# The order of the steady periods of attention: the first values behind the scores, the router's product behind the transposes of q and k

## The chip, the cores and the metric

One core of a Trainium2 chip runs the program. The time is device microseconds of one execution; the time before is the median of three executions, 636.98 us (636.5 to 638.11). A difference of about 0.3% (1.9 us) can be told from none.

## The reference

Attention in chunks of 64 tokens feeds a mixture of experts, where each token goes through one expert of eight:

```python
scores = scale * q_c @ k_c.T           # per batch, head, chunk of 64; head dimension 64
attn = exp(scores - max) / (sum + 1e-9)
out = attn @ v_c                       # 8 x 8 x 576 x 64
x = out as (8, 576, 512)
logits = x @ w_gate; local_gate = sigmoid(x @ w_local)
# e: argmax of the logits, or the previous token's expert where local_gate >= 0.5
h = maximum(x[b, s] @ w1[e], 0)
result[b, s] = softmax(logits)[e] * (h @ w2[e])
```

## The kernel before

The 4608 tokens are cut into 18 blocks of 256. Attention works on several blocks at once, as a pipeline written out by hand: a string of names per stage says in which order the instructions of PE, DVE, ACT and POOL are put into their queues, and each engine runs its queue in that order. The blocks 1 to 15 give fifteen equal periods, which all play the string `PAR["steady"]`; ahead of them stands `PAR["start"]`, behind them `PAR["drain"]`, and then the experts run tile by tile until 638 us.

In period i the names stand for the following (`name*n` takes the next n pieces of that name):

- `s`: the scores of block i+1 (eight pieces of small 64x64 products on PE, L216), then the row maxima on DVE (L227), the subtraction on DVE (L230), the exponential on ACT (L235)
- `va`: the values of block i-1, two halves of four pieces of 64x65 products on PE (L265), each half followed by its division by the row sums on DVE (L277 to L279); both halves use the same PSUM tile `o`, of which there is one
- `tx`: eight 128x128 transposes on PE (L179) of the finished block i-2, in two groups of four; each group fills one of three PSUM tiles `tr`, and ACT copies it out (L169)
- `tq`: sixteen such transposes of q and k of block i+2, in four groups of four, copied out by ACT into `qkT`
- `ra`: the router of block i-2 in four pieces: a product with 32 output rows on PE (L307), a copy `lT` on DVE (L312), two transposes on PE (L316), a reduction on DVE (L321) which four small copies on POOL follow (L325, tile `L`)
- `pr`: four copies on POOL (L171), which pair the heads of block i+3's q and k
- `tp`: eight transposes on PE of the probabilities of block i, two groups, copied out by ACT into `pT`, which the values of the next period read
- `w`: from period 13 on a part of the first expert's weights is split, on ACT (L932) and POOL (L933)
- `lq`, `lv`: the loads of q, k and v for later blocks, on SP's queue
- `h0` to `h3`: in the periods 11 to 15 pieces of the routing of the first 18 tiles, by the numbers in `PAR["hooks"]`: sorting on DVE, small transposes on PE, at the end the one-hot tiles `rh` (L450; six on DVE at h2 of period 14, twelve on POOL at h3), the product of these on PE (L588, h2 of period 15), from which DVE makes the indices and POOL gathers the first tiles of the experts (L627)

```python
    man = tc.manual_schedule(engines=MAN | {ET.Pool})
    for i in range(1, NS - 2):
        play(" ".join(toks), qs4 | {k: v for k, v in opt.items() if v is not None})
```

Period 1 has no `tx` and no `ra`. SP's queue is not in the string's hands: its instructions follow the program.

Of the kernel before, what the change touches and what calls it, by code (L numbers as in the profile page):

```python
# [59 lines left out]
    "t0": "VAVA",  # L60
    "t1": "AAAA",
    "t2": "AVAA",
    "steady": "lq s*8 s h0 tx*8 s va*4 va tq*8 ra*2 h1 tq*8 pr*4 w*4 va*4 lv va ra*2 h2 tp*8 s h3 ",
    "stores": {5: (0,), 6: (1,), 7: (2,), 8: (3,), 9: (4,), 10: (5,), 11: (6,), 12: (7,), 13: (8,), 14: (9,), 15: (10, 11)},
    "hooks": [45, 45, 47, 47, 49, 49, 50, 50, 51, 51, 53, 53, 54, 57, 58, 59, 61, 62, 62],
}
# [1217 lines left out]
```

## Time and profile before

| | |
|---|---|
| median of three runs | 636.98 us |
| the profiled execution, its own time | 640.15 us |
| span of the trace | 638.4 us |
| PE busy | 595.9 us, 93% of the span |
| DVE, ACT, POOL busy | 59%, 50%, 41% |
| granted clock of TensorE, mean | 0.987 of 2.4 GHz |
| steady periods 2 to 15 in the trace | 30.86 to 147.47 us |

The page lists each engine's busy time, groups of instructions and waits. More is read here from the order of time: which instruction an engine starts when, and what ended the idle time ahead of it. Times are counted from the span's start. The trace's counts of matmuls are of issued instructions: a float32 product of 64 columns counts twice, so the 16 products of one half of the values stand as x32.

### The profile page before, as it was taken

Reading aid. Unit: us, or ns where it says so; the run is one execution under the profiler, and the core shown is the slowest. Engines: PE = TensorE matmul, PEld = TensorE weight load, DVE = VectorE, ACT = ScalarE, POOL = GpSimd, SP = SyncE. Lnnn points to the kernel's source line nnn. Section 1 sums busy time; section 2 is a strip of 40 time slices with the busy share of each in tenths; the row PEclk is TensorE's granted clock in tenths of the full one; section 3 lists DMA queues with packets and bytes.
Section 4 is the critical chain, followed back from the end, with each engine's and each line's share of the span. In section 5 each row is a group of like instructions: output and inputs, shape, how many; then the busy total and the mean of one; then the engine's idle time right before and its main releaser. Section 6 shows DMA issues by size and latency. Waiting matters only on the chain. (4 is left out here: it accounts for less than half of the span.)

```text
span 638.4 us, 16143 instructions
## 1 busy us (share of the span) xinstructions
PE 595.9 (93%) x5313; PEld 467.4 (73%) x5313; DVE 378.2 (59%) x813; ACT 318.3 (50%) x546; POOL 263.5 (41%) x559
## 2 busy tenths in 40 slices
PE   4898999888998999999999999999999999999992
PEld 3776887766776878677888786768868688687772
DVE  1665667886686476667535366773666744565330
ACT  2665777656521245675424366653565633545320
POOL 3432433476335234364542353644354445324201
PEclk9998999989998999999999999999999999999997
DMA  9999999998754366597947487969599894559301
GB/s 207 267 215 243 240 283 242 285 251 251 255 179 133 85 101 203 105 310 155 193 97 95 97 208 150 277 144 182 166 138 290 176 198 86 119 169 225 67 18 40
DMA packets 148657, 114.03 MB, mean 179 GB/s; under 512 B 105616, under 2 KB 125072, under 8 KB 148496
## 3 DMA queue, kind: packets, MB, share of 16 engines
q1 hardware_dynamic: 141856, 91.43, 61.5%
q0 software_dynamic: 6640, 20.65, 12.0%
q8 instruction: 77, 1.26, 0.8%
q14 instruction: 84, 0.69, 0.4%
HBM read 77.28 MB, written 20.35 MB: 153 GB/s over the span
## 5 line engine op out<-in xcount | busy, mean ns | idle before, releaser
L700 PE MATMUL y<-w2h,hp 128*128 128x512 f32 x560 | 184.5, 399 | 2.5 <-DVE hp L624 1.0
L686 PE MATMUL h<-w1h,xp 128*128 128x512 f32 x560 | 158.8, 393 | 0.1
L868 POOL DMA_INDIRECT out<-ysb,sidx x41 | 44.1, 1076 | 225.6 <-issue 72.4
L700 PEld LDWEIGHTS y<-w2h,hp 128*128 128x128 f32 x560 | 105.6, 189 | 25.2 <-DVE hp L624 1.4
L686 PEld LDWEIGHTS h<-w1h,xp 128*128 128x128 f32 x560 | 104.1, 188 | 24.8 <-ACTq L1067 1.6
L700 PE MATMUL y<-w2l,hp 128*128 128x512 f32 x280 | 110.0, 393 | 1.4 <-DVEq L1067 1.3
L686 PE MATMUL h<-w1l,xp 128*128 128x512 f32 x280 | 86.7, 391 | 1.5 <-DVEq L1067 1.5
L169 ACT COPY hw<-h 128x512 uint16<-128x512 uint16 x60 | 32.2, 589 | 88.6 <-PE h L686 83.6
L171 POOL COPY qk<-qk 128x512 f32<-128x512 f32 x69 | 40.2, 617 | 60.9 <-issue 31.3
L171 DVE COPY hw<-h 128x512 uint16<-128x512 uint16 x60 | 38.6, 685 | 41.2 <-PE h L686 39.9
L686 PEld LDWEIGHTS h<-w1l,xp 128*128 128x128 f32 x280 | 52.2, 188 | 13.5 <-DVEq L1067 2.2
L700 PEld LDWEIGHTS y<-w2l,hp 128*128 128x128 f32 x280 | 53.0, 189 | 12.3 <-DVEq L1067 2.4
L179 PE MATMUL tr<-ident,qk 128*128 128x128 f32 x288 | 43.7, 299 | 10.9 <-ACT qk L169 5.5
L169 ACT COPY qkT<-tr 128x512 f32<-128x512 f32 x69 | 37.6, 589 | 30.5 <-PE tr L179 25.1
L775 ACT COPY hsb<-ht 128x512 uint16<-128x512 uint16 x58 | 41.5, 775 | 17.6 <-DMA ht<-hw 8.3
L627 POOL DMA_INDIRECT xg<-x_d,gidx x39 | 45.6, 1170 | 9.5 <-issue 4.4
L864 DVE TENSOR_SCALAR ysb<-y,ppr 128x512 f32<-128x512 f32 x35 | 26.2, 749 | 37.5 <-DVEq L1067 21.6
L179 PEld LDWEIGHTS tr<-ident,qk 128*128 128x128 f32 x288 | 34.4, 152 | 18.8 <-POOL qk L171 9.1
L779 DVE SCALAR_TENSOR_TENSOR hp<-hsb,hp 128x512 fp32r<-128x512 f32 x58 | 37.6, 690 | 14.4 <-ACT hp L778 14.4
L106 DVE TENSOR_TENSOR w2l<-raw,w2h 128x1024 fp32r<-128x1024 f32 x28 | 32.5, 1220 | 15.9 <-ACT w2h L105 13.8
L778 ACT ACTIVATE hp<-hsb 128x512 fp32r<-128x512 f32 x58 | 33.5, 623 | 10.1 <-DVE hsb L776 9.0
L227 DVE TENSOR_REDUCE mx<-sc 128x8 f32<-128x512 f32 x36 | 23.1, 684 | 22.5 <-PE sc L216 22.5
(237 smaller groups left out, 872.4 us busy)
## 6 DMA issues: line engine op xcount, KB each, us to landing
raw<-in_moe_w SPq DMA_DIRECT2D x28, 1024.0 KB, 6.4
raw<-in_moe_w SPq DMA_DIRECT2D x16, 512.0 KB, 5.7
qk<-in_q SPq DMA_DIRECT2D x11, 512.0 KB, 6.2
qk<-in_k SPq DMA_DIRECT2D x11, 512.0 KB, 7.1
v<-in_v SPq DMA_DIRECT2D x22, 256.0 KB, 6.1
x_d<-xs SPq DMA_DIRECT2D x7, 521.0 KB, 6.6
x_d<-x_w2h SPq DMA_DIRECT2D x6, 521.0 KB, 6.3
x_d<-x_w2l SPq DMA_DIRECT2D x5, 521.0 KB, 8.1
```

The source lines that it names most:

```text
L106: (lo_eng or nc.vector).tensor_tensor(lo, raw, hi.bitcast(F32), ALU.subtract)
L169: eng.copy(dst, src)
L171: eng.tensor_copy(dst, src)
L179: nc.tensor.transpose(box["ps"][:, n], src_of(n), ident)
L627: nc.gpsimd.indirect_dma_start(out=dst, out_offset=None, in_=src, in_offset=bass.IndirectOffsetOnAxis(ap=gidx[t].bitcast(U32), axis=0))
L686: nc.tensor.matmul(hs[j], xs[a][:, c], W1[w][c][:, 512 * j:512 * j + 512], start=(c == 0 and n == 0), stop=(c == 3 and n == 2))
L700: nc.tensor.matmul(y, hx[f // 4][a][:, f % 4], W2[w][c][:, f % 2, :], start=(f == 0 and n == 0), stop=(f == 7 and n == 2))
L775: nc.scalar.copy(bits[:, j, :, :, 1], ht[:, j, 1])
L778: nc.scalar.activation(hp[j][:, 0], full[:, j], AF.Relu)
L779: V.scalar_tensor_tensor(hp[j][:, 1], full[:, j], 0.0, hp[j][:, 0].bitcast(F32), ALU.max, ALU.subtract)
L864: either(kind and kind[1], lambda: V.tensor_scalar(ysb, y, pr, None, ALU.mult), lambda M: y_part(ysb, y, pr, M), True)
L868: nc.gpsimd.indirect_dma_start(out=out, out_offset=bass.IndirectOffsetOnAxis(ap=sidx[t].bitcast(U32), axis=0), in_=ysb, in_offset=None, bo ...
```

## The change

The string of the steady periods changes, and nothing else. The first half of the values (`va*4`) moves from behind `tx` to right behind the scores; the router's product and its copy (`ra*2`) move from between the two halves of `tq` to behind `pr` and `w`, ahead of the second half of the values; the router's transposes and reduction (the second `ra*2`) move from ahead of the hook h2 to behind `tp`.

```diff
-    "steady": "lq s*8 s h0 tx*8 s va*4 va tq*8 ra*2 h1 tq*8 pr*4 w*4 va*4 lv va ra*2 h2 tp*8 s h3 ",
+    "steady": "lq s*8 s h0 va*4 tx*8 s va tq*8 h1 tq*8 pr*4 w*4 ra*2 va*4 lv va h2 tp*8 ra*2 s h3 ",
```

On PE, in period 2, between the scores of block 3 and the scores that follow (x_w2h is the finished block in its ring buffer, `qk_505` and so on are the four groups of q and k, `pr` the probabilities), there stands before:

```order
L179 MATMUL tr<-ident,x_w2h 128x128 x8
L265 MATMUL o<-v_112,pT 64x65 x16
L179 MATMUL tr<-ident,qk_505 128x128 x4
L179 MATMUL tr<-ident,qk_506 128x128 x4
L307 MATMUL lg<-xT,wg_72 32x256 x4
L179 MATMUL tr<-ident,qk_507 128x128 x4
L179 MATMUL tr<-ident,qk_508 128x128 x4
L265 MATMUL o<-v_112,pT 64x65 x16
L316 MATMUL lg<-ident,lT 128x128 x2
L179 MATMUL tr<-ident,pr 128x128 x8
```

and now:

```order
L265 MATMUL o<-v_112,pT 64x65 x16
L179 MATMUL tr<-ident,x_w2h 128x128 x8
L179 MATMUL tr<-ident,qk_505 128x128 x4
L179 MATMUL tr<-ident,qk_506 128x128 x4
L179 MATMUL tr<-ident,qk_507 128x128 x4
L179 MATMUL tr<-ident,qk_508 128x128 x4
L307 MATMUL lg<-xT,wg_72 32x256 x4
L265 MATMUL o<-v_112,pT 64x65 x16
L179 MATMUL tr<-ident,pr 128x128 x8
L316 MATMUL lg<-ident,lT 128x128 x2
```

The first values now follow the scores without transposes between them, and twenty-four transposes stand in a row; the same holds in every period from 2 to 15.

On DVE, at h2 of period 14 (the second division, the six one-hot tiles, the router's reduction of that period, and the maxima of the next scores), there stands before:

```order
L277 TENSOR_SCALAR rs<-o 128x8
L278 RECIPROCAL rs<-rs 128x8
L279 TENSOR_TENSOR x_w2l<-o,rs 128x2x256
L321 TENSOR_REDUCE x_w2l<-lg 128x2x9
L450 TENSOR_SCALAR rh<-iota_m,rq 128x128 x6
L227 TENSOR_REDUCE mx_2807<-sc_2773 128x8
```

and now:

```order
L277 TENSOR_SCALAR rs<-o 128x8
L278 RECIPROCAL rs<-rs 128x8
L279 TENSOR_TENSOR x_w2l<-o,rs 128x2x256
L450 TENSOR_SCALAR rh<-iota_m,rq 128x128 x6
L321 TENSOR_REDUCE x_w2l<-lg 128x2x9
L227 TENSOR_REDUCE mx_2807<-sc_2773 128x8
```

The reduction has moved behind the one-hot tiles. Likewise in the periods 11 to 15 the copy `lT` (L312) now stands behind the DVE work of h1, where it stood ahead of it. ACT's and SP's queues hold the same instructions in the same order.

## Rows read from the trace of the kernel before

**Rows 1.** Busy time by stretch: length, engines' busy us, granted clock, DMA share, GB/s.

```profile
47.27:58.69 11.42, 9.07 (x171) 7.43 (x170) 5.14 (x14) 5.35 (x10) 3.09 (x8) 0.85 1.02 251
73.15:80.37 7.22, 7.22 (x172) 5.93 (x171) 4.98 (x14) 5.25 (x10) 3.10 (x8) 1.00 0.99 240
102.99:110.47 7.48, 7.48 (x174) 6.09 (x173) 5.97 (x17) 5.52 (x11) 2.97 (x7) 1.00 0.90 204
110.47:119.03 8.56, 7.88 (x176) 6.23 (x175) 7.35 (x23) 5.77 (x12) 3.81 (x11) 1.00 1.12 286
127.61:135.47 7.86, 7.29 (x172) 5.94 (x171) 7.20 (x23) 6.05 (x12) 4.36 (x10) 1.00 1.04 240
```

**Rows 2.** Timeline of PE, period 7: start, us, instruction, count, [idle before <-what ended it].

```profile
73.14 1.16 PE L216 MATMUL sc<-qkT 64*64 64x64 f32 x64
74.24 1.09 PE L179 MATMUL tr<-ident,x_w2l 128*128 128x128 f32 x8
75.26 0.70 PE L265 MATMUL o<-raw,pT 64*64 64x65 f32 x32
75.89 1.09 PE L179 MATMUL tr<-ident,qk 128*128 128x128 f32 x8
76.91 0.64 PE L307 MATMUL lg<-xT,wg 128*32 128x256 f32 x8
77.48 1.09 PE L179 MATMUL tr<-ident,qk 128*128 128x128 f32 x8
78.50 0.70 PE L265 MATMUL o<-raw,pT 64*64 64x65 f32 x32
79.13 0.44 PE L316 MATMUL lg<-ident,lT 128*128 128x128 f32 x2
79.40 1.04 PE L179 MATMUL tr<-ident,pr 128*128 128x128 f32 x8
80.37 0.34 PE L216 MATMUL sc<-qkT 64*64 64x64 f32 x8
```

**Rows 3.** Timeline of PE, period 1, where values follow scores.

```profile
25.05 0.68 PE L265 MATMUL o<-raw,pT 64*64 64x65 f32 x31
```

**Rows 4.** Timeline of ACT, period 7: the copies of two `tr` tiles.

```profile
74.98 1.07 ACT L169 COPY xT<-tr 128x512 f32<-128x512 f32 x2
```

**Rows 5.** Timeline of PE, 26.9 to 51 us: waits early in the kernel.

```profile
26.95 2.33 PE L179 MATMUL tr<-ident,qk 128*128 128x128 f32 x16 [1.23 <-POOL qk L171]
...
40.59 0.71 PE L265 MATMUL o<-v,pT 64*64 64x65 f32 x4
42.17 0.68 PE L265 MATMUL o<-v,pT 64*64 64x65 f32 x28 [0.87 <-DMA v<-in_v]
...
50.53 0.56 PE L216 MATMUL sc<-qkT 64*64 64x64 f32 x19 [2.35 <-issue]
```

**Rows 6.** Timeline of DVE, period 11: first operation of h1, first behind it.

```profile
108.02 0.29 DVE L362 TENSOR_REDUCE mxb<-L 128x18 f32<-128x144 f32 x1
...
110.12 0.16 DVE L277 TENSOR_SCALAR rs<-o 128x8 f32<-128x8 f32 x1
```

**Rows 7.** Timeline of DVE, end of period 14.

```profile
135.81 0.22 DVE L321 TENSOR_REDUCE x_w2l<-lg 128x18 f32<-128x72 f32 x1
135.95 2.20 DVE L450 TENSOR_SCALAR rh<-iota_m,rq 128x128 bf16<-128x128 bf16 x6
```

**Rows 8.** Timeline of POOL, periods 14 and 15.

```profile
137.39 1.05 POOL L325 COPY L<-x_w2l 64x9 f32<-64x9 f32 x4
138.54 7.06 POOL L450 TENSOR_SCALAR rh<-iota_m,rq 128x128 bf16<-128x128 bf16 x12
```

**Rows 9.** Timeline of PE, period 15 and the drain.

```profile
139.08 0.33 PE L216 MATMUL sc<-qkT 64*64 64x64 f32 x4 [2.46 <-issue]
...
146.01 0.60 PE L588 MATMUL tr<-qv,rh 128*128 128x6 bf16 x18
...
158.20 0.63 PE L621 MATMUL tr<-ident,raw 128*128 128x128 f32 x4 [1.37 <-DMA raw<-x_d,gidx]
```

## Prediction, made before the changed kernel ran

> **What bounds the kernel now.** I read the busy times by stretch first, then PE's timeline of one plain period, then every wait of PE from 26 to 160 us, and last the queues that release those waits. A plain period (4 to 10) takes 7.22 us, and PE is busy through all of it, while DVE, ACT and POOL have 5 us of work or less [rows 1]. So PE's own sequence sets the pace there; what the reader is to see in its timeline is that it holds no wait, only blocks of three shapes (128x128 transposes, 64x64 products, the 32-row router product) that alternate [rows 2]. Elsewhere something else is last. In period 3 PE waits for v of block 2 until 42.17, and at 50.53 it has lost 2.35 us to nothing that the profile shows [rows 5]. In period 12 DVE has 7.35 us of work in 8.56 [rows 1]. In periods 14 and 15 POOL's twelve one-hot tiles end at 138.54 + 7.06 = 145.60, and PE uses them at 146.01 [rows 8, 9]. From there a chain over DVE and POOL leads to the gather, for which PE waits 1.37 us at 158.20 [rows 9].
>
> **The change part by part.** No work is added or removed. All of it is order.
>
> *Scores and first values together.* From start to start, the scores with 64 instructions take 74.24 - 73.14 = 1.10 us and a half of the values with 32 takes 75.89 - 75.26 = 0.63 [rows 2]. The difference, 0.47, is what 32 instructions more cost where the shape stays. In period 1, where values follow scores, they run on with no idle time ahead of them [rows 3]. So the two together take 1.10 + 0.47 = 1.57 instead of 1.73, and 0.16 us is saved. Their inputs are there: ACT has copied the probabilities' transposes half a microsecond before, since the scores stand between.
>
> *Twenty-four transposes in a row.* Eight alone take 75.26 - 74.24 = 1.02. The ten of router and probabilities, in a row today, take 80.37 - 79.13 = 1.24 [rows 2]; so a transpose within a row costs 0.11. Twenty-four in a row take 1.02 + 16 x 0.109 = 2.76 instead of 3 x 1.02 = 3.06, and 0.30 is saved. The probabilities and the router's two still stand together, in the other order, at the same 1.24. The router's product now has values behind it, not transposes: its 77.48 - 76.91 = 0.57 [rows 2] I keep. No row shows that neighbour; I bound it by 0.07 either way, what the product's own 0.64 and the 0.57 to the next start lie apart.
>
> *What the row costs.* Three `tr` tiles serve six groups. ACT copies one in 0.59 and starts the next 0.48 later (1.07 for two), its first 74.98 - 74.24 = 0.74 after the row begins [rows 2, 4]; PE makes a group in 4 x 0.109 = 0.44. The fourth group would start at 1.36, its tile is free at 0.74 + 0.59 = 1.33; after that ACT falls behind by 0.05 a group. I take 3 x 0.05 = 0.15. The other end is the sixteen transposes at 26.95, which took 2.33 for four groups [rows 5], 0.56 a group instead of 0.44; they followed POOL's copies, and with their pace the row would lose 5 x 0.12 = 0.6, more than all that is saved. I take the low end, as ACT's copies here are the nearer row.
>
> So a plain period gains 0.16 + 0.30 - 0.15 = **0.31 us** (0.46 at most, a loss of 0.14 at worst), and falls to 6.91.
>
> *Period 3.* The values now come before `tx`, at about 39.1, and v lands just ahead of 42.17, whatever PE does: its load stands in SP's queue in period 1. Today PE does `tx` in that time and waits 0.87 at the end [rows 5]. Now it waits 3 us and does the transposes afterwards. From 42.17 the rest of the values takes 0.5, then the remaining 6.91 - 1.57 = 5.3 of the period: the next scores start at about 48.1, not at 47.27. The lead of period 2 is gone and 0.8 us besides. Seven plain periods (4 to 10) at 0.31 then give 2.2; period 11 begins 1.4 us early.
>
> *Periods 11 to 13.* DVE's work of h1 now stands ahead of `lT`. In period 11 it is 110.12 - 108.02 = 2.1 us [rows 6]; `lT` ends some 7.2 us into the period, the two router transposes were due at 6.6 in a 6.91 period, so PE waits about 0.7 and the period takes 7.8 with the hook's own transposes, against 7.48 [rows 1]: a loss of 0.35. Period 12 goes by DVE, as before; shorter waits for the tile `o` give some 0.45 back (0 to 0.8). Period 13 gains the 0.3 of a plain one. Period 14 starts 1.8 us early.
>
> *Periods 14 and 15.* This is the dearest part. The reduction L321 now stands behind DVE's six one-hot tiles, 2.20 us [rows 7]. POOL's queue holds the four copies that read the reduction, and behind them its twelve one-hot tiles, 7.06 us [rows 8]. Today the reduction starts 135.81 - 127.61 = 8.20 into period 14 and POOL ends the tiles at 145.60, 17.99 into it. Now it starts at 10.4 or, with `lT` late, up to 11; the copies take 1.05, and the tiles end 18.9 to 19.6 into the period: 0.9 to 1.6 lost, I take 1.3. PE came 146.01 - 145.60 = 0.41 late to them [rows 9] because of 2.46 us of waiting at 139.08; now it stands waiting and follows at once, 0.4 won. That wait is over 3 us. The one of 2.35 at 50.53 was followed by a stretch at half clock, 1.2 GHz: period 4 has a granted clock of 0.85 and took 11.42 - 7.22 - 2.35 = 1.85 more than wait and work [rows 1, 5]. The like here costs 1.85, of which the 1.37 that PE waits for the gather covers most: 0.5 lost.
>
> Sum: 1.8 - 1.3 + 0.4 - 0.5 = **0.4 us** gained at the gather. Behind it every stage hangs on PE, 93% busy, and moves with it. Against the profiled execution that is 640.15 - 0.4; that execution is 0.5% above the median of the runs, so I carry the 0.4 to the median: **636.6 us**.
>
> **The rivals.**
>
> *Faster, the wait on nothing goes.* In period 4 PE lost 2.35 and 1.85 of half clock [rows 1, 5]. The profile names no cause; DMA is at 1.02 there. If PE, held in period 3, reaches that place late enough, 4.2 us go: 632.4. For it: the wait is a matter of moments. Against it: the same instructions come in the same traffic.
> What the row shows is a 2.35 us wait of PE in straight-line code. The Trainium skill's page Runtime: NRT & Kernel Launch, section Instruction fetch mechanics, says that instructions are fetched in blocks by DMA while others run, and calls the cost of a block's border mostly hidden. By that rule such a wait would cost nothing and this rival and the one of its like below would go; no row names the fetch, and 2.35 us is not hidden.
>
> *Faster, POOL's chain has room.* If the one-hot tiles are not what PE waits for (the gather's landing then moves with PE), 1.3 + 0.5 come back, and with the full 0.46 a period 7 x 0.15 = 1.0 more: 633.8. Against it: 146.01 follows 145.60 closely [rows 8, 9].
>
> *Slower, half clock at both new waits.* The wait of period 3 becomes 3 us, with but four instructions in it, longer than the 2.35 that drew the half clock. It decides whether it counts as idle as that one did: then 1.85 falls due there, and if the wait for the gather gives no cover at L588, 1.37 more: 636.6 + 3.2 = 639.8.
>
> *Slower, one wait more like that of period 4.* DMA share is 0.9 to 1.12 in these periods [rows 1], and PE uses its instructions 4% faster: 636.6 + 4.2 = 640.8.
>
> *Slower, the row of transposes waits on `tr`.* With the pace of 26.95 nothing of the 0.31 is left in eight periods: 636.6 + 2.5 = 639.1. It decides at 0.46 us of waits a period.
>
> **How the numbers follow.** About 0.3% (1.9 us) is what a measurement can tell, so 635.1 to 638.9 is no change. The forecast has 0.45, with a range of its own of 635.1 to 638.5, from 0.46 or 0.15 a plain period, 0.9 or 1.6 at POOL, 0 or 0.8 in period 12. The first faster rival has 0.15, the second 0.12, the half clock 0.15, one wait more 0.07, the `tr` tiles 0.06. So faster 0.27, same 0.45, slower 0.28. Those of 632.4 and 640.8 lie at the range's edges: 632.3 to 640.2 leaves out half of the first and all of the second with the tails of the others, some 2 in 10.
>
> **What would show it.** A plain period of 6.9 us with scores and values as one block, and PE with no wait ahead of the later groups of the row (else the `tr` rival). PE idle from 39 to 42 us, and the clock's rows behind it. A reduction L321 behind the one-hot tiles, POOL's copies waiting for it, PE waiting over 3 us ahead of L588. Wrong would be a lead at the end of period 13 that arrives in full at the gather, or a plain period that is not shorter.

## The result, and the profile of the changed kernel

The changed kernel takes 646.69 us (median of six runs, 641.53 to 649.52), the kernel before beside it 637.55 (634.54 to 640.02): 1.0135 times as long, 95% interval 1.0085 to 1.0184. It is slower by 9 us, where no change was forecast, and outside the range.

The stretches, as in [rows 1] (length, busy us of PE, PEld, DVE, ACT, POOL, granted clock, DMA share, GB/s), for the periods 3, 4, 5, 10, 12, 13 and 14:

```profile
38.75:51.59 12.84, 10.58 (x171) 9.12 (x170) 5.26 (x13) 5.55 (x11) 3.21 (x8) 0.73 1.08 254
51.59:59.38 7.79, 7.33 (x171) 6.01 (x170) 5.15 (x13) 5.07 (x11) 3.03 (x8) 1.00 0.92 239
59.38:66.40 7.02, 7.02 (x172) 5.83 (x171) 5.21 (x13) 5.07 (x11) 3.04 (x8) 1.00 0.80 228
96.58:107.57 10.99, 8.79 (x171) 7.60 (x170) 5.20 (x13) 5.26 (x11) 3.03 (x8) 0.84 1.01 222
115.30:125.17 9.87, 7.85 (x175) 6.26 (x174) 7.20 (x22) 5.23 (x11) 3.25 (x9) 1.00 1.09 289
125.17:135.64 10.47, 9.04 (x173) 7.73 (x172) 6.65 (x18) 5.74 (x11) 4.16 (x9) 0.84 0.56 147
135.64:145.14 9.50, 7.30 (x171) 5.81 (x170) 9.19 (x23) 7.58 (x14) 6.93 (x12) 1.00 0.83 207
```

A plain period without a wait is indeed shorter, 7.02 instead of 7.22. But period 10, which has the same work, takes 10.99, and 12 and 13 some 10. Two profiles of each kernel (the second ones are of the runs a1 and b1 below) give the sums, in us:

| periods | before | before, second | after | after, second |
|---|---|---|---|---|
| 2 to 4 | 27.83 | 24.42 | 27.58 | 26.42 |
| 5 to 13 | 68.91 | 73.06 | 76.25 | 77.31 |
| 14 and 15 | 19.86 | 18.72 | 21.71 | 21.49 |
| from there to the end | 490.9 | 488.5 | 487.6 | 486.4 |

The profiled executions are 6.7 us apart on the mean. What periods 14 and 15 lose, 2.3 on the mean, the stages behind them give back. The loss that stays is in the periods 5 to 13: 5.8 us on the mean, where the prediction had a gain. PE's timeline shows what it is made of (start, us, instruction, count, [idle before <-what ended it]):

```profile
74.94 0.58 PE L216 MATMUL sc<-qkT 64*64 64x64 f32 x25 [0.56 <-issue]
90.64 0.56 PE L265 MATMUL o<-v,pT 64*64 64x65 f32 x18 [0.86 <-issue]
99.57 0.63 PE L216 MATMUL sc<-qkT 64*64 64x64 f32 x27 [2.20 <-issue]
117.92 0.62 PE L265 MATMUL o<-v,pT 64*64 64x65 f32 x26 [1.34 <-issue]
126.92 0.90 PE L216 MATMUL sc<-qkT 64*64 64x64 f32 x41 [1.17 <-issue]
```

These are waits like that of 50.53 in [rows 5], for nothing that the profile names: 6.13 us in the periods 5 to 13 (7.52 in the second profile), and in each profile two stretches of 3.4 us at half clock (granted 0.5 of 2.4 GHz) behind them, which cost 1.7 each by estimate (half of 3.4). That is 10.2 us on the mean. In the kernel before it is 0.95 and 3.94, and no half clock there. One wait more of each of its profiles belongs to them, though the profile puts it down to DVE:

```profile
101.75 0.44 PE L316 MATMUL lg<-ident,lT 128*128 128x128 f32 x2 [0.41 <-DVE rs L277]
```

```profile
103.94 0.44 PE L316 MATMUL lg<-ident,lT 128*128 128x128 f32 x2 [1.51 <-DVE x_w2h L279]
```

The second is of the second profile, where `lT` was ready at 101.49; the next part shows by the count of instructions what PE waited for. With these two it is 3.4 us on the mean. Waits and half clock taken out, the nine periods last 67.55 and 67.61 us before, 66.72 and 66.39 after. So the change gained 1.0 us there, and 6.8 us more of waits and half clock turn that into the loss of 5.8.

### Where these waits stand

PE's records (matmuls, weight loads, and the waits and other instructions of its sequencer) can be counted from the first. In 20 profiles (both kernels and all the runs below) 98 waits of PE on nothing of 0.15 us and more lie between 30 and 160 us. 96 of them stand at a record that is 193 or 194 past a multiple of 256; the other two lie behind 154 us. The waits at 101.75 and 103.94 stand at 194 too. The profile's table of DMA queues has two rows for instructions, and one of them is (packets, MB, share):

```profile
q8 instruction: 77, 1.26, 0.8%
```

1.26 MB in 77 packets is 16,384 bytes each, 64 for each of 256 instructions, and up to 160 us there is one packet for each such block of PE. The records of packets give, for the profile of the changed kernel and some of the runs below:

```
kernel               PE goes on   wait   packet began ahead of that   after the border before
before                 50.53      2.35   2.78                         5.39
before                139.08      2.46   2.38                         5.71
after                  90.64      0.86   2.29                         2.40
after                  99.57      2.20   2.40                         6.53
after                 126.92      1.17   2.64                         6.36
d3_after_shifted      133.34      5.18   2.53                         6.73
```

In all 96 waits PE goes on 2.2 to 3.3 us (median 2.6) after the block's packet began, and 2.7 us after it at 101.75 and 103.94. In the 17 profiles in which borders and packets pair off one by one, no border is passed less than 2.2 us after its packet began; the medians are 2.7 to 4.0 us. So PE waits there for its own instructions. The Trainium skill, page Runtime: NRT & Kernel Launch, section Instruction fetch mechanics, describes just this, blocks of 256 fetched by DMA while the block before runs, and calls the cost of a border mostly hidden; the blocks agree with the traces, the hiding doesn't where a block is used up in less time than its packet takes to come.

The same count gives how fast PE can use a block. A plain period has 346 records, five of them the sequencer's, so that 256 last 7.02 x 256 / 346 = 5.19 us on the mean, and 7.22 x 256 / 345 = 5.36 before. More has happened to the shortest stretch: taken from any record of the plain periods on, waits left out, 256 records last at least 4.16 us before and 3.10 after. Scores, first values, second values, all rich in instructions, now stand with only the eight transposes of the probabilities and the router's two between them.

### The profile page after: what moved, and what is told of

Its sections match the earlier page's. It is cut to its first block, busy times and chain, and to the rows that moved or that the text cites. A ratio compares the mean times of both kernels' runs of the same rounds, so it can differ in the third digit from the quotient of the medians.

```text
span 645.0 us, 16145 instructions
## 1 busy us (share of the span) xinstructions
PE 597.6 (93%) x5313; PEld 470.4 (73%) x5313; DVE 380.8 (59%) x813; ACT 316.7 (49%) x546; POOL 257.1 (40%) x559
## 3 DMA queue, kind: packets, MB, share of 16 engines
q8 instruction: 77, 1.26, 0.8%
## 5 line engine op out<-in xcount | busy, mean ns | idle before, releaser
L179 PEld LDWEIGHTS tr<-ident,qk 128*128 128x128 f32 x288 | 35.9, 156 | 16.7 <-issue 7.1
L169 ACT COPY xT<-tr 128x512 f32<-128x512 f32 x36 | 19.9, 590 | 36.4 <-PE tr L179 36.4
```

Source lines behind the costliest of these rows:

```text
L169: eng.copy(dst, src)
L179: nc.tensor.transpose(box["ps"][:, n], src_of(n), ident)
```

## The experiments

The first four kernels put each part of the change by itself.

**e1_first_values**: the first values alone are moved.

```diff
-    "steady": "lq s*8 s h0 tx*8 s va*4 va tq*8 ra*2 h1 tq*8 pr*4 w*4 va*4 lv va ra*2 h2 tp*8 s h3 ",
+    "steady": "lq s*8 s h0 va*4 tx*8 s va tq*8 ra*2 h1 tq*8 pr*4 w*4 va*4 lv va ra*2 h2 tp*8 s h3 ",
```

> Of the three moves only the first: the first values follow the scores in every period; the router stands as before. Theory of places (the loss of 8 us lies where the moved work meets something late: v of block 2 in period 3, and DVE's and POOL's queues in the periods 11 to 15): PE waits some 2 to 3 us ahead of the values in period 3, a stretch at half clock behind it, period 3 at 12 us or more instead of 8.8; plain periods at 7.06 (0.16 less); periods 11 to 14 as before; in all 1 to 3 us slower than before. Theory of supply (waits of PE on nothing that the profile shows, behind a full DMA queue, come wherever a plain period gets shorter): besides that, waits on nothing of 3 us or more in sum between 55 and 130 us, where the kernel before has 1.5; 4 to 6 us slower.

Measured: 640.32 against 639.48 us, ratio 1.0024 [0.9987, 1.0060]. Its periods 3 and 4:

```profile
37.90:50.90 13.00, 10.46 (x173) 8.41 (x172) 5.10 (x13) 5.43 (x10) 3.14 (x8) 0.74 1.00 217
50.90:57.90 7.00, 7.00 (x171) 5.84 (x170) 4.90 (x13) 5.10 (x10) 3.08 (x8) 1.00 1.13 307
```

The wait for v and 6.8 us at half clock behind it make period 3 as long as in the changed kernel; period 4 has no wait at its border then, and the two together cost what they cost before (20.22). So period 3 is not the loss.

**e2_router_product** and **e3_router_end**: the router's product alone, its transposes and reduction alone.

```diff
+    "steady": "lq s*8 s h0 tx*8 s va*4 va tq*8 h1 tq*8 pr*4 w*4 ra*2 va*4 lv va ra*2 h2 tp*8 s h3 ",
```

> Of the three moves only the second: the router's product and its copy go behind the sixteen transposes of q and k; the first values and the router's end stand as before. Theory of places: period 3 as before (8.8), plain periods 7.15 to 7.2, since only one change of shape less is paid and tr tiles take a part back; the copy lT behind DVE's hook work makes PE wait 1 to 2 us in the periods 11 to 14 ahead of the router's transposes, which now follow the second values at once; 1 to 3 us slower. Theory of supply: waits on nothing as before (6 us in all), the time within 0.5% of before.

```diff
+    "steady": "lq s*8 s h0 tx*8 s va*4 va tq*8 ra*2 h1 tq*8 pr*4 w*4 va*4 lv va h2 tp*8 ra*2 s h3 ",
```

> Of the three moves only the third: the router's transposes and reduction go behind the transposes of the probabilities. PE's blocks change shape as often as before, so plain periods stay at 7.2. Theory of places: in period 14 the reduction stands behind DVE's six one-hot tiles, POOL's copies wait for it, and the twelve one-hot tiles on POOL end 19 us into the period instead of 18: 1 to 2 us slower. Theory of supply: no change from the plain periods; the time within 0.3% but for that.

Measured: 639.34, 0.9981 [0.9948, 1.0014], and 639.09, 0.9974 [0.9938, 1.0009]. Neither loses. The wait for `lT` is in e2 as long as in the changed kernel, and costs nothing in the end:

```profile
139.06 0.44 PE L316 MATMUL lg<-ident,lT 128*128 128x128 f32 x2 [1.85 <-DVE lT L312]
```

**e4_plain_only**: the new string in the periods 4 to 10, the old one elsewhere.

```diff
+        toks = [t for t in PAR["plain" if 4 <= i <= 10 else "steady"].split() if opt.get(t.split("*")[0], 1) is not None]
```

> The new order in the periods 4 to 10 alone, the old one in 2, 3 and 11 to 15. Theory of places: nothing late is met; plain periods at 7.0, 0.2 less each, so 1.4 us faster than before, or no change by measure; no half clock at 42 us. Theory of supply: the waits on nothing come in these periods, 4 us and more in sum between 55 and 110 us with half clock behind the longest, and the time is 3 to 6 us above the kernel before.

Measured: 641.04, 1.0013 [0.9970, 1.0056]. A plain period takes 7.01, seven of them should give 1.5 us, and nothing arrives: 6.24 us of waits on nothing between 55 and 130 us.

**a1_after_again** is the changed kernel a second time, **e5_from_4** has the new string from period 4 on, so that no wait for v is new.

> The changed kernel once more, beside the others of this call on one chip. Both theories: 6 to 10 us slower than before, a half clock behind period 3's wait, waits on nothing of 4 us or more between 55 and 130 us. If it is within 0.5% of before here, the loss measured first belongs in good part to the spread from execution to execution.

```diff
+        toks = [t for t in PAR["plain" if 4 <= i <= 15 else "steady"].split() if opt.get(t.split("*")[0], 1) is not None]
```

> The new order in the periods 4 to 15, the old one in 2 and 3: period 3 keeps its transposes ahead of the values and needs no 3 us wait. Theory of places with period 3 as the chief loss: no half clock at 42 us, period 3 at 8.8, and 3 to 4 us of the loss of 8 to 9 gone, so 4 to 6 slower than before. Theory of supply: period 4 then has its wait on nothing again (2.35 with half clock), 4.2 us which the changed kernel had not, so nothing is won: 6 to 9 slower than before.

Measured: 646.66, 1.0129 [1.0078, 1.0179], and 646.51, 1.0120 [1.0083, 1.0156]. The whole loss is there without the wait of period 3. (e5's profiled execution, at 640.32, is the fastest of its five; it has 2.99 us of waits on nothing between 55 and 130 us.)

**e6_before_no_v** and **e7_after_no_v**: both orders without the loads of v from block 6 on, to take traffic away.

```diff
+        if i >= 6:
+            return vt
```

> The kernel before without the loads of v from block 6 on (the values of those blocks take what an earlier block left in the buffer, so the output is another), which takes a third of the loaded bytes, and the smallest packets, out of the steady periods. Theory of supply: waits on nothing between 75 and 135 us vanish (under 0.3 us in sum; the kernel before has 1.5 there and 2.46 at 139). Theory of places: they stay, since the instructions and their order do.

> The changed kernel without the loads of v from block 6 on. Theory of supply: waits on nothing between 75 and 135 us vanish here too, the plain periods 7 to 10 are all 7.0, and of the 8 us of loss against the pair's other kernel 4 to 6 go. Theory of places: against the pair's other kernel it loses 6 to 9 us as with the loads, half of it in period 3, which these loads don't touch, and the rest in the periods 11 to 15.

Measured: 651.17 and 656.46. Tokens are routed otherwise here, so only the two are compared: the new order loses 5.3 us, instead of the 8 of a1. Its waits on nothing fall to 3.83 us between 55 and 130 us (2.64 in e6), but they don't go, which is a miss: without these loads the packets are still late at times.

**c1_new_from_11**, **c2_first_values_from_4**, **c3_end_ahead_of_hook**, **c4_product_ahead_of_hook**: the new string in 11 to 15 alone; the first values alone, from 4 on; the changed kernel with `ra*2` ahead of h2 again; the changed kernel with, from 11 on, the product ahead of h1 again.

```diff
+        toks = [t for t in PAR["other" if i >= 11 else "steady"].split() if opt.get(t.split("*")[0], 1) is not None]
```

> The old order in the periods 2 to 10, the new one in 11 to 15: the other half of the run that had the new order in 4 to 10 and lost nothing by measure. Theory of places (the loss lies where the new order meets the routing's work on DVE and POOL): this alone loses 5 to 8 us, with period 14 at 9.3 to 9.5 and the one-hot tiles' products ending 19.5 us into it. Theory of a sum (shorter plain periods bring the later ones into a fuller DMA queue, and only both together lose): 0 to 3 us slower.

```diff
+    "other": "lq s*8 s h0 va*4 tx*8 s va tq*8 ra*2 h1 tq*8 pr*4 w*4 va*4 lv va ra*2 h2 tp*8 s h3 ",
```

> Only the first values move, and only in the periods 4 to 15: period 3 keeps its cover, the router keeps its place. Theory of places: plain periods 7.06, no queue on DVE or POOL is later than before: 1 to 3 us faster than before. Theory of supply: period 4 has its wait on nothing and its half clock, the plain periods get waits on nothing of 2 us or more, and the time is within 0.3% of before.

```diff
+    "steady": "lq s*8 s h0 va*4 tx*8 s va tq*8 h1 tq*8 pr*4 w*4 ra*2 va*4 lv va ra*2 h2 tp*8 s h3 ",
```

> The changed kernel with the router's transposes and reduction back ahead of the hook h2 in every period: the reduction stands ahead of DVE's one-hot tiles again, the copy lT stays behind the hook's work. Theory that the reduction behind the one-hot tiles is the loss: POOL's tiles end 1 to 2 us sooner in period 14, and at least 4 of the 8 us of loss go. Theory that lT behind the hook's work is the loss: PE waits for lT as long or longer in the periods 11 to 14, and 6 to 9 us of loss stay.

```diff
+    "other": "lq s*8 s h0 va*4 tx*8 s va tq*8 ra*2 h1 tq*8 pr*4 w*4 va*4 lv va h2 tp*8 ra*2 s h3 ",
```

> The changed kernel, but in the periods 11 to 15 the router's product and its copy lT stand ahead of the hook h1 again, between the halves of the transposes; the reduction stays behind the one-hot tiles. Theory that lT behind the hook's work is the loss: PE has no wait for lT, period 14 falls from 9.4 to under 8, and at least 4 of the 8 us of loss go. Theory that the reduction is the loss: 6 to 9 us stay.

| | us | ratio | on nothing, 55 to 130 us |
|---|---|---|---|
| c1 | 638.44 | 1.0003 [0.9966, 1.0039] | 1.72 |
| c2 | 639.27 | 1.0055 [1.0021, 1.0090] | 6.12 |
| c3 | 643.31 | 1.0077 [1.0035, 1.0119] | 4.44 |
| c4 | 645.29 | 1.0110 [1.0038, 1.0181] | 7.36 |

c1 has the late one-hot tiles in full, and loses nothing:

```profile
140.08 0.88 POOL L326 COPY L<-x_w2l 64x9 f32<-64x9 f32 x4 [2.64 <-DVE x_w2l L322]
141.07 7.03 POOL L451 TENSOR_SCALAR rh<-iota_m,rq 128x128 bf16<-128x128 bf16 x12
```

They end 148.10 - 129.0 = 19.1 us into its period 14, instead of 17.99 [rows 8]. c4 has no wait for `lT` (its period 14 takes 7.05) and loses as much as the changed kernel. So no place that the prediction named is the cause by itself. The waits on nothing, with those at a border that the profile puts down to another engine (c1 has one of 1.65), can be compared over the fifteen profiles with the usual instructions in the periods 4 to 10 (those above without e6 and e7, and b1, d3 and d4 below). They are 5.6 us on the mean where the first values stand behind the scores in the periods 4 to 10 (nine profiles: 2.6 to 7.5), and 3.7 where not (six: 1.4 to 6.2). The two ranges overlap, and the sum of one profile goes only loosely with the time: c2 and e4 have over 6 us and lose 3.5 and 0.8.

The loss is not a sum of the parts either. e4 and c1 have between them the whole of e5's order and lose 0.8 and 0.2 us, e5 loses 7.7; e1, e2 and e3 are the three moves, and none loses by itself. Why the loss needs them together is not shown.

The next four ask what the waits hang on.

**d3_after_shifted** and **d4_before_shifted**: 64 products of one column ahead of the start string, 128 records more.

```diff
+        first = ps_tr.tile([P, 4, P], F32, name="tr")
+        for _ in range(64):
+            nc.tensor.matmul(first[0:1, 0, 0:1], ones[:, 0:1], ones[:, 0:1], start=True, stop=True)
```

> The changed kernel, with 64 products of one column on PE ahead of the start string (128 records of matmul and weight load more, some 5 to 10 us of PE where it has nothing else to do; no other work changes). In all kernels so far each wait of PE on nothing stands at a record that is 193 or 194 past a multiple of 256, counted from the first. Theory A (a border of blocks of 256): here too, so that in the string the waits stand 128 records earlier or later than before, at other instructions; their sum between 55 and 130 us may come out anywhere from 2 to 9 us. Theory B (places in the order): they stay at the same instructions, which are then at 65 or 66 past a multiple of 256, with the sum of 7 us. Whole time 640 to 650 by A, 646 by B.

> The kernel before with the same 64 products of one column ahead of the start string. Theory A: its waits on nothing stand at 193 or 194 past a multiple of 256 again, that is not ahead of the scores at 50.5 us but half a block away; sum between 55 and 130 us 1 to 5. Theory B: at 50.5 us again, 65 past a multiple. Whole time 634 to 643 by A, 637.5 by B.

Measured: d3 645.48, 1.0104 [1.0055, 1.0153]; d4's four executions lie from 635.74 to 647.74, the profiled one at 642.83, too far apart for a comparison with the 638.68 (634.79 to 640.98) of the kernel before. All thirteen waits on nothing in the two profiles are again at 193 or 194 past a multiple of 256, at other instructions of the string, half a block away. Of d4:

```profile
56.84 0.98 PE L179 MATMUL tr<-ident,x_w2l 128*128 128x128 f32 x7 [1.95 <-issue]
...
128.58 0.92 PE L216 MATMUL sc<-qkT 64*64 64x64 f32 x24 [3.39 <-issue]
```

and of d3:

```profile
133.34 0.69 PE L265 MATMUL o<-raw,pT 64*64 64x65 f32 x10 [5.18 <-issue]
```

In d4 there is no wait at 50.53 any more. The waits go by the count, not by the place in the order. The old order has 6.2 us of them between 55 and 130 us here, as many as the new one. That the shift made them more is not shown: b1, the old order unshifted, has 5.5 by the same count.

**f1_before_wide** and **f2_after_wide**: both orders with half the score instructions, of double width.

```diff
-            for cp in range(2):
-                ch = 2 * cp + cc
-                for j in range(2):
+            for cp in range(2):
+                for j in range(2 - 2 * cc):
...
-                        sc[j][64 * cp:64 * cp + 64, h, cc, :],
-                        of(0, j, h, ch),
-                        of(1, j, h, ch),
+                        sc[j][64 * cp:64 * cp + 64, h].rearrange("p c k -> p (c k)"),
+                        of(0, j, h, 2 * cp),
+                        of(1, j, h, 2 * cp, 128),
```

> The kernel before, but each pair of 64x64 products of the scores (two chunks of the same head pair) is one product of 64x128 with the first chunk's q: the same columns, half the instructions. The second chunk's scores are not what the reference asks for, so other tokens go to other experts, and only the time up to 150 us and the comparison with the kernel of the changed order in the same form say something. In a plain period this takes 64 matmul and weight-load records out of some 341; 256 records then last (7.2 - 0 to 0.4) x 256 / 277 = 6.3 to 6.7 us instead of 5.4. Theory A (PE's waits on nothing are blocks of 256 instructions that arrive late, because the new order uses them faster): the waits on nothing between 55 and 130 us fall from some 2 us to under 0.5, and the wait of 2.35 us in period 4 goes or halves. Theory B (they hang on the places in the order, or on traffic alone): they stay near 1.5 to 2.5 us. Whole time: 634 to 650, by the other routing, no difference between the theories.

> The changed kernel with the same wide scores (the second chunk's scores are not the reference's). 256 records last (7.0 - 0 to 0.4) x 256 / 277 = 6.1 to 6.5 us instead of 5.26. Theory A: its waits on nothing between 55 and 130 us fall from 7 us to under 1; no stretch at half clock behind them; from the scores of period 4 to those of period 14 it is 1 to 2 us faster than the same form of the kernel before, and the whole is within 2 us of it or faster, with period 3's 4 to 5 us the only loss (if that also goes, faster by 2). Theory B: the waits stay at 4 to 8 us, periods 8, 10, 12 and 13 of 8 to 11 us, and the whole is 5 to 9 us slower than the same form of the kernel before.

Measured: 634.71 (633.78 to 638.38) and 636.32 (632.81 to 640.93). The new order now loses 1.6 us, not 9 (the two route tokens alike, but otherwise than the kernel before). A period of each without waits, f1 first:

```profile
61.80:69.00 7.20, 7.20 (x140) 5.78 (x138) 5.02 (x14) 5.29 (x10) 3.07 (x8) 1.00 1.09 287
```

```profile
59.40:66.40 7.00, 7.00 (x141) 5.78 (x141) 5.25 (x13) 5.12 (x11) 3.04 (x8) 1.00 1.07 261
```

The DMA share is as high as ever, the period hardly shorter, 140 matmuls instead of 172. f1 has no wait on nothing at all between 30 and 160 us; f2 has 1.91 between 55 and 130 (1.24 more at 131.1), where under 1 was expected, and 3.15 in all instead of 6.59. From the scores of period 4 to those of period 14 it takes 74.9 us and f1 73.5, where 1 to 2 us less was expected, so the plain periods' gain doesn't arrive even here. f2's period 3 still takes 12.8 us (v late, half clock), which f1's 8.6 doesn't; more than the 1.6 us is in that one place, in a profiled execution (640.15) near the top of its ten.

**f3_before_more** has the old order with 32 products of one column more in each period; **b1_before_again** is the kernel before once more.

```diff
+                for _ in range(4):
+                    nc.tensor.matmul(box["ps"][0:1, 0, 0:1], ones[:, 0:1], ones[:, 0:1], start=True, stop=True)
```

> The kernel before, with four products of one column on PE ahead of each group of four 128x128 transposes (they write into the tile that the transposes then fill, so nothing is computed otherwise): 32 products in a plain period, 64 records of matmul and weight load more, 405 instead of 341. If one costs 10 to 30 ns, a plain period takes 7.5 to 8.2 us and 256 records last 4.8 to 5.2 us instead of 5.4, less than in the changed order. Theory A (blocks of 256 instructions that come late): waits on nothing at 193 or 194 past a multiple of 256, more of them than the 6.3 us of the kernel before between 30 and 160 us (9 to 20), with more stretches at half clock, and beyond what the products cost the whole loses 3 to 15 us. Theory B (the place in the order): the order is the old one, so the waits stay at 3 to 6 us and the whole is later by the products' own time alone.

> The kernel before once more, for a second profile. Theory A: the same places modulo 256 (193 or 194), so the waits of PE on nothing stand ahead of some of the same instructions, but not all of the same blocks; 3 to 8 us in all between 30 and 160 us, and the execution's time follows that sum. Theory B: at 50.5 and 139 us as in the first profile, with the same lengths.

Measured: f3 662.77, 1.0363 [1.0264, 1.0461]; b1 639.53. f3's expectation missed, and its reason is instructive. The products cost 62 ns each, (9.22 - 7.22) / 32, more than the 10 to 30 supposed; so 256 records last 9.2 x 256 / 405 = 5.8 us, longer than before, and there is no wait on nothing at all. One of its periods:

```profile
51.80:61.00 9.20, 9.20 (x203) 7.00 (x202) 5.08 (x12) 5.66 (x9) 3.17 (x9) 1.00 0.88 223
```

More instructions in the old order, and the waits are gone: their number alone doesn't make them. The shortest 256 records last 4.54 us here, 5.60 in f1. The traffic is thinner too (a share of 0.83 from 60 to 120 us, 0.99 in the kernel before from 58.69 to 95.30), and the packets begin a median 1.5 us after the border before them, at most 3.7; in the four profiles of the two kernels the medians are 2.5 to 3.1 and the latest 5.5 to 7.1. f1, with full traffic and no wait, speaks for the pace of instructions; f3 alone doesn't tell it from that of data. Nor is the pace all: f2's shortest 256 records last 5.42 us, longer than f3's, and f2 still has its 1.91 under fuller traffic.

b1 has 7.41 us of waits on nothing between 30 and 160 us, 6.33 in the first profile, partly at other borders:

```profile
50.46 0.56 PE L216 MATMUL sc<-qkT 64*64 64x64 f32 x19 [1.55 <-issue]
68.02 0.57 PE L265 MATMUL o<-v,pT 64*64 64x65 f32 x20 [1.15 <-issue]
...
86.42 0.93 PE L179 MATMUL tr<-ident,qk 128*128 128x128 f32 x7 [1.50 <-issue]
```

The same border at 50.5 is late in both, those at 68 and 86 in the second alone. So one profile of such a kernel is not enough to count them.

No order that was tried is shown to be faster than the kernel before.

## Why the prediction was wrong

*Scores and first values together: right.* A plain period of the changed kernel, as in [rows 2]:

```profile
59.38 1.16 PE L216 MATMUL sc<-qkT 64*64 64x64 f32 x64
60.36 0.65 PE L265 MATMUL o<-v,pT 64*64 64x65 f32 x32
60.94 1.09 PE L179 MATMUL tr<-ident,x_w2l 128*128 128x128 f32 x8
61.87 2.16 PE L179 MATMUL tr<-ident,qk 128*128 128x128 f32 x16
63.96 0.64 PE L307 MATMUL lg<-xT,wg 128*32 128x256 f32 x8
64.53 0.70 PE L265 MATMUL o<-v,pT 64*64 64x65 f32 x32
65.16 1.09 PE L179 MATMUL tr<-ident,pr 128*128 128x128 f32 x8
```

The two take 60.94 - 59.38 = 1.56; 1.57 was forecast. The router's product costs 0.57, as kept.

*Two small slips, on which nothing hangs.* ACT's work in a plain period is 5.25 us, not 5 or less [rows 1], and 42.17 + 0.5 + 5.3 is 48.0, not 48.1.

*The row of transposes: mis-sized.* It takes 63.96 - 60.94 = 3.02, not 2.91; what the `tr` tiles cost is 0.26, not 0.15. ACT ends its first three copies at 62.28, 62.77 and 63.26, as early as forecast, but PE starts the fourth, fifth and sixth group 0.14 after them, at 62.42, 62.91 and 63.40, and the sum had no term for that. So the gain is 7.22 - 7.02 = 0.20 a period, not 0.31.

*The wait on nothing: the step that failed.* It was taken as one event at one place, of 4.2 us, which either goes, stays or comes once more, the last with a chance of 0.07 and PE's 4% as its only reason. It is a border that comes every 256 instructions, some 20 times in the attention, at each of which a packet is late or not; the changed order has more of them late, in both profiles of each kernel. The sentence that it was "a matter of moments" and the rule of the Trainium skill's page were both weighed against the one row, without counting the instructions between the four such waits that the trace of before held (50.5, 126.0, 131.0, 139.1: record 193 or 194 past a multiple of 256 each). The plain periods' gain was then carried to the end at 0.31 x 7, though a shorter period also uses up PE's blocks faster; f1 and f2, whose blocks last longer, differ by 1.6 us instead of 9. By the sums above, 6.8 us of waits and half clock were added in the periods 5 to 13, and 1.0 gained.

*Period 3: both rivals, at once.* PE waits for v as forecast, though 2.3 us and not 3, in three pieces:

```profile
41.10 0.30 PE L265 MATMUL o<-v,pT 64*64 64x65 f32 x2 [1.19 <-DMA v<-in_v]
41.85 0.33 PE L265 MATMUL o<-v,pT 64*64 64x65 f32 x2 [0.45 <-DMA v<-in_v]
42.80 1.13 PE L265 MATMUL o<-v,pT 64*64 64x65 f32 x28 [0.62 <-DMA v<-in_v]
...
45.62 3.60 PE L179 MATMUL tr<-ident,qk 128*128 128x128 f32 x16
```

The half clock that one rival priced at 1.85 runs for 6.8 us and costs 3.4: sixteen transposes take 3.60 instead of 2.16. In exchange the wait of period 4 shrinks to 0.46, as another rival had it. Periods 3 and 4 together take 20.63 us, 20.22 before. In the second profile (a1) it went the other way: PE waits 1.2 us for v, no half clock follows, period 3 takes 8.84, and the wait of period 4 stays, 1.86 with 3.4 us at half clock behind it. Which of the two comes differs from one execution to the next.

*Periods 11 to 13: DVE's part about right, PE's not.* PE waits 0.28 for `lT` in period 11 (0.7 forecast) and none of note in 12 and 13; these periods lose 3.1 us, on the mean of two profiles each, in the first profile mostly by the waits on nothing at 117.92 and 126.92 and the half clock behind the second.

*Periods 14 and 15: right in place and nearly in size.* DVE and POOL in period 14 and behind it:

```profile
141.61 1.29 DVE L446 CAST rq<-ri 128x36 f32<-128x36 int32 x1
142.82 1.30 DVE L912 TENSOR_SCALAR qsA<-oh 128x18 f32<-128x18 bf16 x1
...
144.31 0.42 DVE L312 COPY lT<-lg 128x256 f32<-128x256 f32 x1
...
145.68 1.06 DVE L450 TENSOR_SCALAR rh<-iota_m,rq 128x128 bf16<-128x128 bf16 x6
146.65 0.23 DVE L321 TENSOR_REDUCE x_w2l<-lg 128x18 f32<-128x72 f32 x1
```

```profile
141.57 2.51 POOL L933 TENSOR_TENSOR w1l<-raw,w1h 128x512 fp32r<-128x512 f32 x2 [0.44 <-ACT w1h L932]
146.94 0.88 POOL L325 COPY L<-x_w2l 64x9 f32<-64x9 f32 x4 [2.85 <-DVE x_w2l L321]
147.92 7.03 POOL L450 TENSOR_SCALAR rh<-iota_m,rq 128x128 bf16<-128x128 bf16 x12
```

The reduction starts 146.65 - 135.64 = 11.0 into the period, POOL waits 2.85 for it, and its tiles end at 154.95, 19.3 into it: "10.4 or up to 11" and "18.9 to 19.6" were forecast. On PE:

```profile
144.78 0.44 PE L316 MATMUL lg<-ident,lT 128*128 128x128 f32 x2 [1.80 <-DVE lT L312]
...
155.01 0.18 PE L588 MATMUL tr<-qv,rh 128*128 128x6 bf16 x1 [0.40 <-POOL rh L450]
...
166.16 0.63 PE L621 MATMUL tr<-ident,raw 128*128 128x128 f32 x4 [0.18 <-DMA raw<-x_d,gidx]
```

PE waits for the tiles one by one, 2.5 us in all and not one wait of over 3, with half clock behind them; the wait for the gather, 1.37 in [rows 9], is 0.18. From the start of period 14 to L621 it is 30.5 us, 30.6 before: the cover that the prediction counted on (the 1.37, and the 2.46 of waiting on nothing at 139.08, which this profile doesn't have) took all of it. c1 says the same.

## What to carry to other kernels

A wait for nothing in straight-line code is worth a count of the engine's instructions before it is called chance: where several stand at one remainder of 256, and in the instruction queue a packet began 2 to 3 us ahead of the end of each, the engine outruns its instructions, and an order that is shorter on paper can give its gain back there. Look at such a border also for waits that the profile puts down to another engine. Price such an order by the time that its shortest 256 instructions last as well as by the period. And profile both kernels more than once, since the places of these waits change from one execution to the next.

## What the runs showed of the hardware that was not expected

- PE's blocks of 256 instructions, 16,384 bytes each, with waits of 0.15 to 5.18 us at their borders under a DMA share of about 1, and 3.4 or 6.8 us at half clock behind many of the longer ones.
- A small DVE operation beside POOL's split of the weights takes as long as one operation of POOL: L912 needs 1.30 us while POOL's two of L933 take 2.51, and 0.16 in the kernel before, where the two don't meet (POOL's pair begins at 134.95 there):

```profile
134.42 0.16 DVE L912 TENSOR_SCALAR qsA<-oh 128x18 f32<-128x18 bf16 x1
```

  The six one-hot tiles take 1.06 us now that they miss it, 2.20 in [rows 7]. The Trainium skill, page SBUF — State Buffer, section SBUF: two separate sides, has an exclusive lock between a GpSimd operation and a VectorE operation that runs in a two-port mode or has two SBUF inputs, for the whole of an instruction. The trace agrees: L446 and L912 take 1.29 and 1.30, the time of one of POOL's two each; whether they ran in such a mode no run shows.
- 32 products of one column, 62 ns each in f3, cost a plain period 2.0 us.

What stays open: what makes a given packet late. That traffic has a part in it is argued from f3 and e7, where it is thinner and the waits are fewer, but in both something else changes with it; and whether the mean pace (5.19 instead of 5.36 us a block) or the shortest stretch (3.10 instead of 4.16) does more of the harm was not told apart. That the changed order has more late packets than the old one is shown for these two kernels, by two profiles each and by f1 and f2; why neither half of the periods and none of the three moves brings the loss by itself stays open too.
